# Batch 0's v as one contiguous load, loads in the order q, k, v, and 512-column gap filling

## The chip, the cores and the metric

The kernel runs on one core of one Trainium2 chip. Its time is the device time of one execution in microseconds (us). Three executions of the kernel before gave 324.27, 326.92 and 322.95 us, a median of 324.27.

Engines are TensorE (PE in the profile; its weight loads are PEld), VectorE (DVE), ScalarE (ACT), GpSimd (POOL) and SyncE (SP). Each takes its instructions in order. DMAs are issued here from two queues: GpSimd's, which can change a type on the way (float32 to bf16), and SyncE's.

## What is computed

An attention whose keys and values are first mixed block by block, and then a two-layer network on its result. Sizes: 4 batches, 8 heads, a sequence of 768 in 8 blocks of 96, head dimension 64; 3072 tokens of 512, a hidden layer of 2048.

```python
P = sort_net                                   # (4, 8, 8, 8)
for _ in range(5):                             # Sinkhorn
    P = exp(P - max(P, -1))
    P = P / (sum(P, -1) + 1e-9)
    P = P / (sum(P, -2) + 1e-9)
k_sorted = einsum('bhij,bhjcd->bhicd', P, k_blocks)
v_sorted = einsum('bhij,bhjcd->bhicd', P, v_blocks)
attn = softmax(q_block @ k_sorted_block.T / 8)   # within each block of 96
x = (attn @ v_sorted_block)                      # to (3072, 512)
h = x @ w_in
out = (max(h, 0) + alpha * min(h, 0)) @ w_out
```

## The kernel before

**Order of the work.** Every operation is added to a graph (`G.add`, with an engine, a cost in ns, what it reads and writes, and a priority, the smaller the sooner). `_Graph.schedule` (L88) is a planner: it puts the operations of each engine into a fixed order by its own costs and due times, of DMAs too. Operations marked EITHER go to ScalarE or VectorE as it decides. `emit` writes that order out, with semaphore waits. On the chip each engine then follows its order, whatever the real times are. `fill` (L153) puts extra matmuls, whose result nobody reads, into the gaps that the plan has on TensorE up to a given time (`warm`, L817).

**Loads.** GpSimd issues in this order: v, k, q of batch 0 (768 KB each as they land in bf16), the two weight matrices (`w_in` in four parts, `w_out` in two), zeroing of QN, then k, q (eight pieces, QN) and v of later batches. For batch 0, `load_v` (L362) reads v in halves: 128 partitions, each with 3072 numbers, from source rows taken in two interleaved sets of 64.

**Batch 0.** Sinkhorn (L421) runs on 32 rows, with the exp on ScalarE (L431) and the rest on VectorE. `spread_k` (L445) lays P out on 128 partitions and masks it to a block matrix BDK; `spread_v` (L461) does so for BDV, whose third part belongs to batch 0's v. `prep_k` and `prep_q` (`pairs`, L477) multiply KS by BDK, or QS by an identity, 16 matmuls a unit for six units, which sorts and transposes at once; the copies to KT and QTz follow (L318 is the copy on either engine). `conv_v` (L512) reorders v in SBUF from VST to VD in four pieces, and `prep_v` (L518) sorts it in eight units of 16 matmuls over 64 partitions each, with BDV; its copies go to VS.

**Later batches.** q comes by DMA into QN and is transposed by DMA on SyncE's queue (`turn_q`, L349, L351) into QTz, of which there are two; the next batch's QN loads wait for those transposes. v is sorted on TensorE by `sort_v` (L538, L545), written to DRAM and read back in another order (`turn_v`, L554; L556 and L563, SyncE's queue) into VS, in two halves. k goes the way of batch 0.

**Attention and FFN.** `attention` (L571) does one block g of 32: scores (L594, or L591 for later batches), their negated maximum (L598), scores again with the maximum subtracted (L622 or L612, and L604), exp to Esb (L632), the product with VS (L640), division (L647, L650), transposition into xT (L659). `ffn1` (L671, matmuls L679) and `ffn2` (L699, matmuls L711) work on finished tokens between the blocks, by priority.

Of the kernel before, what the change touches and what calls it, by code (L numbers as in the profile page):

```python
# [7 lines left out]
AP = bass.AP  # L8
# [48 lines left out]
class _Graph:  # L57
# [30 lines left out]
    def schedule(self):  # L88
# [22 lines left out]

        free = dict.fromkeys(ENGS, 0.0)
        dma_free = 0.0
        order = {e: [] for e in ENGS}
# [38 lines left out]
    def fill(self, make, unit, first, before):  # L153

        out, last = [], self.ops[first].end + 300
        for op in self.order["pe"]:
            n = int((op.start - last) * 0.9 / unit)
            if op.start < before and n > 2:
                x = _Op("pe", lambda e, n=n: make(e, n), n * unit, 0.0, None, len(self.ops))
                x.start, x.end = last, last + n * unit  # L160
                x.deps.add(first)
                self.ops.append(x)
                out.append(x)
            out.append(op)
            last = max(last, op.end)
        for pos, op in enumerate(out):
            op.pos = pos
        self.order["pe"] = out
# [69 lines left out]
def bass_sinkhorn_attn__then__act_prelu_kernel(  # L238
# [37 lines left out]
    selk = sb("selk", [32, 4, 128], F32)  # L276
    selv = sb("selv", [32, 3, 128], F32)
    dtmp = sb("dtmp", [128, 64], F32)
    dsel = sb("dsel", [128, 8], F32)
    BDK = sb("BDK", [128, 4, 128], BF16)  # L280
    BDV = sb("BDV", [128, 3, 128], BF16)
    epst = sb("epst", [32, 8], F32)
# [30 lines left out]
    BANK_H = [(psH, x * 512, 1024, [("psH", x, 0), ("psH", x, 1)]) for x in range(2)]  # L313
    BANK_O = [(psO, x * 512, 1024, ["psO%d" % x]) for x in range(2)]
    BANKS0 = [BANK_P] + BANK_H + BANK_O

# [45 lines left out]
    def load_v(b, prio):  # L362
        if b == 0:
            G.add(POOL, lambda e: e.dma_start(
                AP(VST, 0, [[6144, 128], [1, 3072]]),
                AP(v.tensor, 0, [[3072, 2], [6144, 64], [1, 3072]])),
                load_us, w=[("VST", 0), ("VST", 1)], prio=prio, dma=(d_v[0], 0))
            return
        G.add(POOL, lambda e: e.dma_start(
            AP(VST, (b % 2) * 64 * 6144, [[6144, 64], [1, 6144]]),  # L370
            AP(v.tensor, b * HB, [[6144, 64], [1, 6144]])),
            load_us, w=[("VST", b % 2)], prio=prio, dma=(d_v[b], 0))


    def consts():
# [29 lines left out]
        red(mvj[:, :], AP(identf, 0, [[128, 128], [1, 8], [8, 16]]), "mvj")  # L405
        for t, w, ld, name in ((selk, 16, 512, "selk"), (selv, 8, 384, "selv")):
            G.add(ACT, lambda e, t=t, w=w, ld=ld: copy(e, AP(t, 0, [[ld, 32], [w, 32], [1, w]]),
                                                       AP(identf, 0, [[128, 32], [1, 32], [0, w]])), 600,
                  r=["identf"], w=[name], prio=-66)
        G.add(ACT, lambda e: copy(e, AP(selv, 256, [[384, 32], [64, 2], [8, 8], [1, 8]]),  # L410
                                  AP(identf, 0, [[128, 32], [0, 2], [1, 8], [0, 8]])), 300,
              r=["identf"], w=["selv2"], prio=-66)
        return ib.idx
# [47 lines left out]
    def spread_v(x, prio):  # L461
        G.add(PE, lambda e: e.matmul(psYP[:, 1, 0:64], AP(selv, x * 128, [[384, 32], [1, 128]]), P32[:, :]),
              500, r=["P"] + (["selv2"] if x == 2 else ["selv", ("xT", 1)]), w=PSP, prio=prio)
        G.add(DVE, lambda e: e.tensor_tensor(
            out=AP(dtmp, 0, [[64, 128], [8, 8], [1, 8]]), in0=AP(psYP, 512, [[1024, 128], [8, 8], [1, 8]]),
            in1=AP(mvj, 0, [[8, 128], [0, 8], [1, 8]]), op=AluOpType.mult), 210,
            r=PSP + ["mvj"], w=["dtmp"], prio=prio)
        G.add(DVE, lambda e: e.reduce_sum(dsel[:, :], AP(dtmp, 0, [[64, 128], [8, 8], [1, 8]]),
                                          axis=AxisListType.X), 200, r=["dtmp"], w=["dsel"], prio=prio)
        G.add(DVE, lambda e: e.tensor_tensor(  # L470
            out=AP(BDV, x * 128, [[384, 128], [8, 16], [1, 8]]),
            in0=AP(mvh, 0, [[16, 128], [1, 16], [0, 8]]),
            in1=AP(dsel, 0, [[8, 128], [0, 16], [1, 8]]), op=AluOpType.mult), 290,
            r=["dsel", "mvh"], w=[("BDV", x)], prio=prio)

# [22 lines left out]
    def prep_k(b, u, prio, bank=BANK_P):  # L498
# [8 lines left out]
        if b == 0 and u == 1:  # L507
            G.add(DVE, lambda e: e.tensor_copy(AP(KT[0], 48, [[ld, 128], [bk, 32], [1, 16]]),
                                               AP(KT[0], 0, [[ld, 128], [bk, 32], [1, 16]])), 500,
                  r=[("KT", 0, 0), ("KT", 0, 1)], w=["KTpad"], prio=prio + 1)  # L510

    def conv_v(u, prio):  # L512
        o = AP(VD, 16 * u * 64, [[6144, 128], [64, 16], [1, 48]])
        i = AP(VST, 16 * u, [[6144, 128], [1, 16], [64, 48]])
        G.add(EITHER if u == 3 else ACT, lambda e: copy(e, o, i), {"act": 1520, "dve": 890},
              r=[("VST", 0), ("VST", 1)] + ["P"] * (u == 3), w=[("VD", u)], prio=prio)

    def prep_v(u, prio, bank):  # L518
        t, off, row, keys = bank

        def f(e):
            inst = None
            for dd in range(8):
                for th in range(2):
                    inst = e.matmul(AP(t, th * 64 * row + off + dd * 64, [[row, 64], [1, 64]]),
                                    AP(VD, th * 64 * 6144 + (8 * u + dd) * 64, [[6144, 64], [1, 64]]),
                                    AP(BDV, th * 64 * 384 + 256 + th * 64, [[384, 64], [1, 64]]))
            return inst
        G.add(PE, f, 8 * 33, r=[("VD", u // 2), "VD0", ("BDV", 2)], w=keys, prio=prio)
        o = AP(VS[0], 8 * u, [[64 * 65, 112], [65, 64], [1, 8]])  # L530
        i = AP(t, off, [[row, 112], [1, 64], [64, 8]])
        G.add(EITHER, lambda e: copy(e, o, i), {"act": 685, "dve": 690}, r=keys + [("VS1", 0)], w=[("VS", 0)] if u == 0 else
              [("VSu", u)], prio=prio)
# [4 lines left out]
    def sort_v(bs, c, prio):  # L538
        row, rows, keys = (bs[0] % 2) * 64, 64 * len(bs), [("VST", b % 2) for b in bs]

        def f(e):
            inst = None
            for b in bs:
                r0 = (b % 2) * 64
                inst = e.matmul(AP(psYP, r0 * 1024 + 512, [[1024, 64], [1, 512]]),  # L545
                                AP(BDV, r0 * 384 + (b // 2) * 128 + r0, [[384, 64], [1, 64]]),
                                AP(VST, r0 * 6144 + c * 512, [[6144, 64], [1, 512]]))
            return inst
# [19 lines left out]

    first_y = []

    def attention(g, prio):  # L571
        b, i = g // NB, g % NB
        n, m = b % 2, g % 2
        far = b > 0
# [9 lines left out]
        def s1(e):  # L584
# [11 lines left out]
            return inst  # L596
        G.add(PE, s1, t_pe(*[(96, 96)] * 8), r=kt_keys + qt_keys, w=banks_s, prio=prio)
        G.add(DVE, lambda e: e.tensor_reduce(  # L598
            AP(nm[m], 0, [[8, 96], [4, 2], [1, 4]]), AP(psX, 0, [[1024, 96], [512, 2], [96, 4], [1, 96]]),
            AxisListType.X, AluOpType.max, negate=True), t_dve(768), r=banks_s, w=[("nm", m)], prio=prio)  # L600

# [6 lines left out]
        def s2(e):  # L608
# [17 lines left out]
            for h4 in range(4):  # L626
# [3 lines left out]
        G.add(PE, s2, t_pe(*[(192, 96), (96, 96), (96, 96)] * 4), r=kt_keys + qt_keys + [("nm", m), "identb"],  # L630
              w=banks_s, prio=prio)
        G.add(ACT, lambda e: e.activation(  # L632
            AP(Esb[m], 0, [[768, nk], [384, 2], [1, 384]]), AP(psX, 0, [[1024, nk], [512, 2], [1, 384]]),
            ACTF.Exp, scale=0.125), t_act(768), r=banks_s, w=[("Esb", m)], prio=prio)

        def o(e):
# [6 lines left out]
            return inst  # L643
        op = G.add(PE, o, t_pe(*[(65, 96)] * 8), r=vs_keys + [("Esb", m)], w=banks_o, prio=prio)
        if g == 1:
            first_y.append(op)
        G.add(DVE, lambda e: e.reciprocal(AP(rec[m], 0, [[8, 96], [4, 2], [1, 4]]),  # L647
# [75 lines left out]


    load_v(0, -98)
    load_k(0, -97)
    load_q(0, -96)
    ident_op = consts()
    sinkhorn()
    for u in range(4):  # L730
        conv_v(u, -50)
    bank = 0
    spread_k(0, -48)
    spread_v(2, -47.5)
    for name, count, prio in (("k", 6, -47), ("v", 8, -45), ("q", 6, -46)):
        for u in range(count):
            x = BANKS0[bank % 5]
            bank += 1
            prep_k(0, u, prio, x) if name == "k" else prep_v(u, prio, x) if name == "v" else prep_q(u, prio, x)
    for p in range(4):  # L740
# [76 lines left out]
    def warm(e, n):  # L817
        inst = None
        for _ in range(n):
            inst = e.matmul(psYP[:, 0, 0:128], identb[:, :], identb[:, :])  # L820
        return inst
    G.fill(warm, 56, ident_op, first_y[0].start)
    if __import__("os").environ.get("SCHED"):
# [39 lines left out]
```

## Time and profile before

| | us |
|---|---|
| median of three executions | 324.27 |
| the profiled execution | 322.16 |
| its span, first to last instruction | 320.4 |
| TensorE busy (matmul) in it | 274.1 |
| VectorE, ScalarE, GpSimd busy | 170.9, 139.3, 34.6 |
| first sorting matmul of P (L447) starts | 38.84 |
| first product with VS (L640) starts | 64.13 |
| first FFN matmul (L679) starts | 68.69 |

Stages, from the busy time of each engine in windows of the span:

| window, us | TensorE busy | granted clock | GB/s moved |
|---|---|---|---|
| 0 to 10 | 6.36 | 1.00 | 114 |
| 10 to 20 | 5.23 | 0.90 | 206 |
| 20 to 30 | 0.00 | 0.50 | 195 |
| 30 to 40 | 1.16 | 0.50 | 196 |
| 40 to 50 | 6.72 | 0.67 | 167 |
| 60 to 65 | 4.95 | 0.77 | 31 |
| 70 to 75 | 5.00 | 0.50 | 22 |
| 90 to 120 | 28.79 | 1.00 | 145 |
| 120 to 160 | 34.13 | 0.91 | 134 |
| 160 to 200 | 39.69 | 1.00 | 89 |
| 250 to 300 | 49.64 | 1.00 | 33 |

In the profile an entry such as "VD<-VST" is what is written and what is read; "x6" counts instructions; a bracket gives the idle time before an instruction and what ended it. In the DMA views the last number is the time from issue to landing. The time slices give the busy share in tenths; PEclk is the granted TensorE clock in tenths of full speed, and GB/s counts the bytes as they are written. The chain of waits is followed back from the last instruction, at each step to what released it.

### The profile page before, as it was taken

What the parts mean: (1) busy time and instruction counts of PE and PEld (TensorE: products, weight loads), DVE (VectorE), ACT (ScalarE), POOL (GpSimd) and SP (SyncE); (2) the same over time, 40 slices, a digit from 0 to 9 for tenths busy, and PEclk for the clock granted to TensorE, in tenths of its full rate; (3) what the DMA queues carried; (4) which work ended last, traced back from release to release, by engine and by line L of the source; (5) the groups of instructions that cost most, each with busy time, mean ns of one, the idle gap of its engine ahead of it and who ended that gap; (6) DMA issues with size and microseconds to landing.
All of it is one profiled execution on the core that took longest, in us unless ns stands there. A gap on an engine that the chain in (4) does not pass through costs nothing.

```text
span 320.4 us, 6603 instructions
## 1 busy us (share of the span) xinstructions
PE 274.1 (86%) x2871; PEld 182.7 (57%) x2904; DVE 170.9 (53%) x349; ACT 139.3 (43%) x265; POOL 34.6 (11%) x53
## 2 busy tenths in 40 slices
PE   5900176989899893999999999999999999999996
PEld 5800165866666551766666666666666666655542
DVE  5100443375676523677675666677656666554420
ACT  4000542242577652576545445544444544444421
POOL 8920050000061006200000000000000000000000
PEclk9965565685999997899999999999999999999999
DMA  6999999226999999949937991000000000000012
GB/s 89 208 196 205 192 168 164 44 27 39 142 124 140 132 199 166 178 101 52 170 45 136 106 110 46 35 34 2 35 33 35 33 36 33 35 33 35 33 55 78
DMA packets 66589, 29.81 MB, mean 93 GB/s; under 512 B 58032, under 2 KB 62144, under 8 KB 66368
## 3 DMA queue, kind: packets, MB, share of 16 engines
q1 hardware_dynamic: 41552, 15.75, 35.1%
q0 software_dynamic: 25008, 13.64, 32.2%
q8 instruction: 23, 0.38, 0.6%
q14 instruction: 6, 0.05, 0.1%
HBM read 29.64 MB, written 8.65 MB: 119 GB/s over the span
## 4 chain that ended last, share of the span: by engine, by line
PE 77%; DMA 12%; SPq 3%; issue 3%; DVE 2%; ACT 1%; POOLq 0%
PE psH L679 26%; PE psYP L711 21%; DMA VST<-in_v_dram 10%; PE psS L604 4%; PE psO L640 4%; SPq L351 3%; PE psS L711 3%; PE psS L591 3%; PE psS L612 3%; PE psYP L485 2%; PE psYP L545 2%; DMA VS<-v_sorted_dram 2%; PE psYP L820 2%; PE psO L659 2%; PE psS L622 1%
## 5 line engine op out<-in xcount | busy, mean ns | idle before, releaser
L690 DVE SCALAR_TENSOR_TENSOR hT<-t,omaT,psH 128x384 bf16<-128x384 f32 (+1 forms) x144 | 80.5, 566 | 60.6 <-ACT t L687 59.3
L679 PE MATMUL psH<-xT,w_in_bf 128*128 128x384 bf16 (+1 forms) x576 | 103.1, 314 | 0.0
L687 ACT ACTIVATE t<-psH 128x384 f32<-128x384 f32 (+1 forms) x144 | 64.7, 453 | 68.2 <-PE psH L679 67.4
L711 PE MATMUL psYP<-w_out_bf,hT 128*128 128x512 bf16 x304 | 80.1, 382 | 2.4 <-issue 1.0
L679 PEld LDWEIGHTS psH<-xT,w_in_bf 128*128 128x128 bf16 x576 | 50.8, 100 | 26.5 <-issue 1.8
L711 PEld LDWEIGHTS psYP<-w_out_bf,hT 128*128 128x128 bf16 x336 | 30.9, 98 | 27.8 <-issue 1.2
L632 ACT ACTIVATE Esb<-psS 96x768 bf16<-96x768 f32 (+1 forms) x31 | 25.0, 807 | 33.8 <-PE psS L604 33.4
L598 DVE TENSOR_REDUCE nm<-psS 96x8 bf16<-96x768 f32 x31 | 29.5, 950 | 9.6 <-PE psS L591 6.3
L344 POOL DMA_DIRECT2D QN<-in_q_dram x24 | 19.8, 857 | 62.5 <-DMA QTz<-QN 62.5
L604 PE MATMUL psS<-identb,nm 96*96 96x96 bf16 (+1 forms) x248 | 23.7, 214 | 0.0
L604 PEld LDWEIGHTS psS<-identb,nm 96*96 96x96 bf16 (+1 forms) x248 | 21.7, 129 | 2.0
L447 PE MATMUL psYP<-P,selk 32*128 32x64 f32 x8 | 2.5, 406 | 23.6 <-DVE P L442 23.6
L820 PE MATMUL psYP<-identb 128*128 128x128 bf16 x229 | 19.1, 256 | 3.6 <-ACT identb L318 3.6
L640 PEld LDWEIGHTS psO<-VS,Esb 96*96 96x96 bf16 (+1 forms) x248 | 15.9, 129 | 11.0 <-DMA VS<-v_sorted_dram 5.7
L650 DVE TENSOR_TENSOR xq<-psO,rec 96x512 bf16<-96x512 f32 x31 | 21.3, 687 | 1.1
L640 PE MATMUL psO<-VS,Esb 96*96 96x65 bf16 (+1 forms) x248 | 16.7, 213 | 5.9 <-DMA VS<-v_sorted_dram 5.4
L820 PEld LDWEIGHTS psYP<-identb 128*128 128x128 bf16 x229 | 16.9, 116 | 4.1 <-ACT identb L318 3.6
L612 PE MATMUL psS<-QTz,KT 128*96 128x192 bf16 x96 | 19.1, 254 | 0.1
L318 ACT ACTIVATE outstg<-psYP 128x512 f32<-128x512 f32 x21 | 12.5, 597 | 8.8 <-PE psYP L711 8.8
L447 PEld LDWEIGHTS psYP<-P,selk 32*128 32x128 f32 x8 | 1.8, 275 | 24.4 <-DVE P L442 23.8
L318 ACT ACTIVATE VD<-VST 128x768 bf16<-128x768 bf16 x3 | 4.5, 1490 | 25.7 <-DMA VST<-in_v_dram 25.7
L433 DVE TENSOR_REDUCE rs<-P 32x8 f32<-32x64 f32 x5 | 1.0, 208 | 26.6 <-ACT P L431 26.6
(117 smaller groups left out, 234.4 us busy)
## 6 DMA issues: line engine op xcount, KB each, us to landing
out_dram<-outstg SPq DMA_DIRECT2D x24, 256.0 KB, 2.0
VST<-in_v_dram POOLq DMA_DIRECT2D x4, 768.0 KB, 33.1
KS<-in_k_dram POOLq DMA_DIRECT2D x4, 768.0 KB, 36.5
QN<-in_q_dram POOLq DMA_DIRECT2D x24, 96.0 KB, 6.2
v_sorted_dram<-VD SPq DMA_DIRECT2D x6, 384.0 KB, 4.4
VS<-v_sorted_dram SPq DMA_DIRECT2D x6, 384.0 KB, 10.1
w_in_bf<-in_moe_w_in_dram POOLq DMA_DIRECT2D x4, 512.0 KB, 42.1
w_out_bf<-in_moe_w_out_dram POOLq DMA_DIRECT2D x2, 1024.0 KB, 52.6
```

The lines of the kernel that those rows point to most:

```text
L344: G.add(POOL, lambda e, h=h: e.dma_start(AP(QN, h * 128 + (h // 4) * 64, [[6144, 128], [1024, 6], [1, 64]]), AP(q.tensor, b * HB + h * S * ...
L598: G.add(DVE, lambda e: e.tensor_reduce(AP(nm[m], 0, [[8, 96], [4, 2], [1, 4]]), AP(psX, 0, [[1024, 96], [512, 2], [96, 4], [1, 96]]), Axis ...
L604: return e.matmul(AP(psX, (p // 4) * 512 + (p % 4) * 96, [[1024, nk], [1, 96]]), AP(nm[m], p, [[8, 96], [0, nk]]), AP(identb, 0, [[128, 96 ...
L612: e.matmul(AP(psX, (h4 // 2) * 512 + (h4 % 2) * 192, [[1024, 96], [1, 192]]), AP(KT[n], (h4 * 8 + i) * 96, [[ld, 128], [1, 96]]), AP(QTz[n ...
L632: G.add(ACT, lambda e: e.activation(AP(Esb[m], 0, [[768, nk], [384, 2], [1, 384]]), AP(psX, 0, [[1024, nk], [512, 2], [1, 384]]), ACTF.Exp ...
L640: inst = e.matmul(AP(psZ, hp * 512 + h4 * 68, [[1024, 96], [1, 65]]), AP(Esb[m], pos(h4, hp) * 96, [[768, nk], [1, 96]]), AP(VS[n], ((hp * ...
L650: G.add(DVE, lambda e: e.tensor_tensor(out=AP(xq[m], 0, [[512, 96], [256, 2], [64, 4], [1, 64]]), in0=AP(psZ, 0, [[1024, 96], [512, 2], [6 ...
L679: inst = e.matmul(AP(psH, hb * 512, [[1024, 128], [1, n]]), AP(w_in_bf, kt * DFF + ft * 128, [[KT_TILES * DFF, 128], [1, 128]]), AP(xT, kt ...
L687: G.add(ACT, lambda e: e.activation(AP(t1[tb], 0, [[384, 128], [1, n]]), AP(psH, hb * 512, [[1024, 128], [1, n]]), ACTF.Relu, scale=-1.0), ...
L690: G.add(DVE, lambda e: e.scalar_tensor_tensor(out=AP(hT, ft * RING + tok % RING, [[FT_TILES * RING, 128], [1, n]]), in0=AP(t1[tb], 0, [[38 ...
L711: inst = e.matmul(AP(bank[0], bank[1], [[row, 128], [1, 512]]), AP(hT, ft * RING + tok % RING, [[FT_TILES * RING, 128], [1, 128]]), AP(w_o ...
L820: inst = e.matmul(psYP[:, 0, 0:128], identb[:, :], identb[:, :])
```

## The change

- `load_v` reads batch 0's v with the source as 128 rows of 3072 in their order. v is then laid out as k is, so that `prep_v` sorts it with BDK, over all 128 partitions in one matmul, each second column of BDK being taken; BDV's third part, its selector and its `spread_v` go.
- The loads of batch 0 are issued in the order q, k, v; q's preparation comes first in priority, then k's, the scores of the first two blocks, v's conversion (all four pieces now on either engine), and v's sorting, which uses four PSUM banks.
- In the planner GpSimd starts at 400 ns, so that its order changes a little. `fill` begins at 5000 ns, fills any gap in which a matmul has room, with 512-column matmuls costed at 215 ns (128 columns and 56 ns before), and ends before the first `prep_v` that writes the bank the filler writes, where it ended before the second block's product with VS.

```diff
@@ schedule
         free = dict.fromkeys(ENGS, 0.0)
+        free["pool"] = 400.0
@@ fill
-            n = int((op.start - last) * 0.9 / unit)
-            if op.start < before and n > 2:
+            n = int((op.start - max(last, 5000)) * 0.9 / unit)
+            if op.start < before and n > 0:
@@ load_v
-                AP(v.tensor, 0, [[3072, 2], [6144, 64], [1, 3072]])),
+                AP(v.tensor, 0, [[3072, 128], [1, 3072]])),
@@ conv_v
-        G.add(EITHER if u == 3 else ACT, lambda e: copy(e, o, i), {"act": 1520, "dve": 890},
-              r=[("VST", 0), ("VST", 1)] + ["P"] * (u == 3), w=[("VD", u)], prio=prio)
+        G.add(EITHER, lambda e: copy(e, o, i), {"act": 1520, "dve": 890},
+              r=[("VST", 0), ("VST", 1)], w=[("VD", u)], prio=prio)
@@ prep_v
                 for th in range(2):
                     inst = e.matmul(AP(t, th * 64 * row + off + dd * 64, [[row, 64], [1, 64]]),
-                                    AP(VD, th * 64 * 6144 + (8 * u + dd) * 64, [[6144, 64], [1, 64]]),
-                                    AP(BDV, th * 64 * 384 + 256 + th * 64, [[384, 64], [1, 64]]))
+                                    AP(VD, (8 * u + dd) * 64, [[6144, 128], [1, 64]]),
+                                    AP(BDK, th, [[512, 128], [2, 64]]))
-        G.add(PE, f, 8 * 33, r=[("VD", u // 2), "VD0", ("BDV", 2)], w=keys, prio=prio)
+        op = G.add(PE, f, 8 * 33, r=[("VD", u // 2), "VD0", ("BDK", 0)], w=keys, prio=prio)
+        if keys == ["psY"]:
+            first_y.append(op)
@@ attention: scores, maximum and exp of the first two blocks get the priority ps_
+        ps_ = g / 8 - 46.5 if g < 2 else prio
@@ the main part
-    load_v(0, -98)
+    load_q(0, -98)
     load_k(0, -97)
-    load_q(0, -96)
+    load_v(0, -96)
     ident_op = consts()
     sinkhorn()
+    spread_k(0, -48)
+    for u in range(6):
+        prep_q(u, -50, BANKS0[u % 5])
+    for u in range(6):
+        prep_k(0, u, -47, BANKS0[(u + 1) % 5])
     for u in range(4):
-        conv_v(u, -50)
-    bank = 0
-    spread_k(0, -48)
-    spread_v(2, -47.5)
-    for name, count, prio in (("k", 6, -47), ("v", 8, -45), ("q", 6, -46)):
-        for u in range(count):
...
+        conv_v(u, -45.5)
+    for u in range(8):
+        prep_v(u, -45, (BANK_O + [BANK_P, BANK_Y])[u % 4])
@@ warm
-            inst = e.matmul(psYP[:, 0, 0:128], identb[:, :], identb[:, :])
+            inst = e.matmul(psYP[:, 0, :], identb[:, :], AP(identb, 0, [[128, 128], [0, 4], [1, 128]]))
-    G.fill(warm, 56, ident_op, first_y[0].start)
+    G.fill(warm, 215, ident_op, first_y[0].start)
```

## The prediction, made before the change was run

> **What bounds the kernel now.** I read the page first: the time slices and the chain of work that ended last.
>
> ```profile
> PE   5900176989899893999999999999999999999996
> ...
> PEclk9965565685999997899999999999999999999999
> DMA  6999999226999999949937991000000000000012
> GB/s 89 208 196 205 192 168 164 44 27 39 142 124 140 132 199 166 178 101 52 170 45 136 106 110 46 35 34 2 35 33 35 33 36 33 35 33 35 33 55 78
> ```
>
> A slice is 8.0 us. From the eleventh on, the sixteenth apart, TensorE is full at a full clock, so a microsecond saved before that is a microsecond at the end unless a later wait takes it back. Slices 3 to 5 are nearly empty: they are the place to look. The chain in order of time:
>
> ```profile
> 1.32 32.47 DMA VST<-in_v_dram
> 33.80 1.50 ACT VD L318
> 38.84 0.68 PE psYP L447 x2
> ...
> 45.98 3.28 issue
> ...
> 54.61 1.92 issue
> ...
> 120.26 6.95 DMA VS<-v_sorted_dram
> 127.25 0.85 PE psO L640 x8
> ```
>
> It starts with batch 0's v, 32.5 us for 768 KB. The timeline shows what else that held up:
>
> ```profile
> 33.80 1.50 ACT L318 ACTIVATE VD<-VST 128x768 bf16<-128x768 bf16 x1 [25.74 <-DMA VST<-in_v_dram]
> 35.21 0.24 ACT L431 ACTIVATE P<-P 32x64 f32<-32x64 f32 x1
> 35.35 1.49 ACT L318 ACTIVATE VD<-VST 128x768 bf16<-128x768 bf16 x1
> ```
>
> ScalarE's fixed order has v's conversion ahead of Sinkhorn's fourth exp, so P, whose first three rounds end at 9.6 us at 1.81 us a round, is ready only at 38.8. Why the load is slow shows in the DMA issues, window by window:
>
> ```profile
> VST<-in_v_dram POOLq DMA_DIRECT2D x1, 768.0 KB, 32.5
> KS<-in_k_dram POOLq DMA_DIRECT2D x1, 768.0 KB, 35.2
> QS<-in_q_dram POOLq DMA_DIRECT2D x1, 768.0 KB, 37.9
> KS<-in_k_dram POOLq DMA_DIRECT2D x1, 768.0 KB, 53.7
> ```
>
> Issued at 1.32, 2.25, 3.16 and 13.10, they land at 33.8, 37.4, 41.1 and 66.8. k and q come 3.65 us behind their forerunner; v took nine times that. With all 16 DMA engines at work the slices show about 200 GB/s, 12.5 each; at 60 to 66 us the windows show 26 to 33, two engines' worth, while late loads are still landing. So v (source [[3072,2],[6144,64],[1,3072]]) runs on two engines, 393 KB on each, and every later load has a share that queues behind them.
> The Trainium skill, DMA: Bandwidth & Descriptors, "Why a DMA increments its semaphore by 16 and not by 1", says that the number of engines is the largest up to 16 that divides both slowest dimensions: 2 here. It also knows an exception in which GpSimd's copies use 16 anyway; by that v would land like k, and the change would gain nothing from its load. The 32.5 us speak against the exception.
>
> **The load.** As [[3072,128],[1,3072]] it has the form of k's and q's, 3.65 us. Two engines lose 393 − 49 = 344 KB each, at 49/3.65 = 13.5 KB per us 25.5 us. The fixed part is 32.5 − 393/13.5 = 3.3 us. So q lands at 1.32 + 3.3 + 3.65 = 8.3, k at 11.9, v at 15.6. What follows comes 25.5 us earlier: the last w_in at 28.1 (53.6), w_out at 37.6 (63.1), batch 1's k at 41.3.
>
> **Start to first FFN matmul** (L679 at 68.69 now). P no longer stands behind v: two more rounds of 1.81 from 9.6 give 13.2, up to 15 with q's copies (0.60 to 0.69 each) between; I take 14.3. spread_k to BDK took 38.84 to 40.36: 15.9. q's six units are then done. Six k units, copies 0.65 on two engines, with latency: KT at 18.5. First scores, reduction 0.95, second scores 0.9, exp 0.81: about 23. Conversions of v (1.5 on ScalarE, 0.8 on VectorE) fill in from 15.6 on. prep_v changes form: 128 matmuls contract over 128 rows, where now pairs of 64-row ones ran beside each other at 27 ns each (32 in 0.87 us). Nearest rows: L591, 128-row with 96 columns, 8 in 0.36 us, 45 ns; L604, 8 in 0.45. At 45 ns this is 5.8 us, at 27 it is 3.5; I take 45, since they can't pair. Its copies, 8 x 0.69 on two engines, 2.8 us, lie beside it. The first L640 comes at about 26. Add one stall like the "issue" ones, 3.28 and 1.92 us, which lie 128 matmuls apart while DMA is full: 0 to 5, I take 2. So 28; L679 followed L640 by 4.6: 32.6. Gain 36 us, between 32 and 40.
>
> **Small parts.** spread_v(2) goes: 0.69 us of TensorE, 0.74 of VectorE, 0.3 of ScalarE; all counted above as absent. The order q, k, v puts v last, 7.3 us behind q, where P and k's copies cover it; without them 7 us are at stake. The start of 400 in the planner and BDV's narrower rows move nothing by themselves. **Filler:** 170 matmuls of 128 columns ran at 12 per us first, 22 from 8 us on; four times as long that is 0.33, then 0.18 us each, planned at 0.215 for 90% of each gap. A planned gap of 3 us before q can overrun to about 4.2, ending near 9.2 and not 8: covered by Sinkhorn (14.3). If P were earlier, at most some 3 us. Warm against cold clock in this stretch: 0 to 3 us gain, taken as nil since copies set most of it.
>
> **Where a stall goes.** At 121.8 TensorE waits 5.4 us for batch 1's second half of VS, whose load stands behind batch 2's transposes on SP:
>
> ```profile
> 75.57 13.12 SPq L351 DMA_TRANSPOSE QTz<-QN  x6
> ...
> 107.60 12.61 SPq L351 DMA_TRANSPOSE QTz<-QN  x6
> 120.26 0.58 SPq L563 DMA_DIRECT2D VS<-v_sorted_dram  x1
> ```
>
> That chain is paced by queues: batch 1's q landed, transposes, GpSimd's next q loads from 90.81 to 97.39, their landing 5.2, transposes 12.7, VS 7.0. From the first transpose: 15.2 + 6.6 + 5.2 + 12.7 + 7.0 = 46.7 us; now it takes 51.7, because it also waits some 5 us for batch 0's last scores. Its start moves with the loads, not with the first matmul: 75.6 − 25.5 = 50.1, or 47 if all eight QN loads go ahead of batch 1's v, which waits on GpSimd for the conversions (till about 21; they now end at 39.6). VS then lands at 94 to 97. TensorE arrives at 121.8 − 36 = 85.8. The stall becomes 8 to 11 where it was 5.4: +2.8 to +5.6. I take 2.8, as TensorE's order can put more FFN work ahead of it. Batch 1's v lands near 51, where its first sort (86.4 − 36 = 50.4) wants it: 0 to 3, inside that stall. Sum: −36 + 2.8 = −33.2.
>
> **The numbers.** Against the profiled execution (320.4 span, 1.8 around it, 322.16) this gives 289.0. The median shown is 2.1 higher; I predict **290**.
>
> **Rivals.**
> 1. *The queue chain does not bind.* If the planner puts VS ahead of batch 2's transposes, the stall disappears: −36 − 5.4 = −41.4, 281 to 283. For: those two stand only 10 us apart in SP's order. Against: the orders of SP are made by the same costs. 0.2.
> 2. *It binds harder.* v_sorted's second write also falls behind the transposes, as its sort waits for v while scores come sooner: another 4.4 us of landing and 0.5 to 1 of issue, or a start 4 us slower: −26, about 298. 0.22.
> 3. *The load isn't what is slow*, 33 us being the bandwidth for all 6.5 MB queued. Then q's transposes still start at 75.6, the stall hands all back: 318 to 324. Against: 26 GB/s at the end. 0.04.
> 4. *Slower: the clock.* At 70 to 78 us TensorE was busy 2.00 of every 2.00 us and had a clock of 0.50. Fill now ends before v's preparation, in front of the FFN. Half clock costs half of the work done under it; to be slower than before it has to last over 2 x 33 = 66 us, 80 for 2%; the longest busy stretch seen is about 9. Worth 330. 0.03.
>
> The skill's TensorE: Matmul & The Clock Gate, Part 1, has the full clock back after about 3.4 us of sustained work; the eight busy microseconds at 0.50 differ from that. By it, rival 4 couldn't be.
>
> My case holds 0.51. 80% lie in **279 to 301**, which reaches from rival 1 with a 2 us better start to rival 2 with a 3 us worse one. What can be told from no change is about 2%, 6.5 us. Faster 0.93 (my case, rivals 1 and 2), within 2% 0.04, slower 0.03.
>
> **What would show it.** Right: landings near 8, 12 and 16 us; P by 15; L447 before 17; first L679 at 30 to 35; no stretch at 26 to 33 GB/s before 60 us; transposes from 47 to 51; one wait for VS of 8 to 11 us before 100. Wrong: v landing after 30 (the engines' reading falls); first L679 after 40 (filler, the 128-row matmuls or code loading were underpriced); a wait for VS above 15 or none; half clock for tens of microseconds in the FFN.

## The result, and the profile after

The changed kernel takes 302.88 us (median of four, 301.19 to 303.34) against 324.42 of the kernel before: 0.9326 of it, 95% interval 0.9265 to 0.9386, so 21.5 us less. 290 was predicted, with 279 to 301 as the range: the gain is there, but more than a third of what was forecast is missing. The profiled execution has a span of 299.5 us, 20.9 less than before.

First the landings of the first three loads (DMA issues of the changed kernel in the window 1 to 4 us; the last number is from issue to landing):

```profile
QS<-in_q_dram POOLq DMA_DIRECT2D x1, 768.0 KB, 6.6
KS<-in_k_dram POOLq DMA_DIRECT2D x1, 768.0 KB, 9.7
VST<-in_v_dram POOLq DMA_DIRECT2D x1, 768.0 KB, 13.0
```

Issued at 1.30, 1.96 and 2.81, they land at 7.9, 11.7 and 15.8; 8.3, 11.9 and 15.6 were predicted. Batch 1's k lands at 41.2 (41.3). The page's time slices, 7.5 us each:

```profile
PE   5996999999960049999999999999999999999995
...
PEclk9997559999995559999999999999999999999999
...
GB/s 121 207 206 189 215 169 214 177 166 105 129 189 88 188 191 27 125 73 155 40 131 149 64 84 35 38 2 35 37 35 37 11 27 35 37 35 35 37 70 70
```

The hole at the beginning is gone. There is a new one in slices 12 to 15, which the kernel before does not have in that size. TensorE's timeline shows its edges, with the idle time and its cause in the bracket:

```profile
87.28 0.52 PE L593 MATMUL psS<-KT,QTz 128*96 128x96 bf16 x8
108.65 0.63 PE L548 MATMUL psYP<-VST,BDV 64*64 64x512 bf16 x2 [20.84 <-DMA VST<-in_v_dram]
```

L548 is the sort of later batches' v (L545 before); this is the first one for batches 2 and 3. It does not wait for VS, as the prediction had it, but for batch 3's v in VST. GpSimd's timeline says why that v is late:

```profile
20.50 0.68 POOL L361 DMA_DIRECT2D KS<-in_k_dram  x1
21.35 1.06 POOL L371 DMA_DIRECT2D VST<-in_v_dram  x2 [0.17 <-issue]
66.15 6.62 POOL L346 DMA_DIRECT2D QN<-in_q_dram  x8 [43.73 <-DMA QTz<-QN]
86.66 6.56 POOL L346 DMA_DIRECT2D QN<-in_q_dram  x8 [13.89 <-DMA QTz<-QN]
93.14 0.62 POOL L371 DMA_DIRECT2D VST<-in_v_dram  x1
```

Before, GpSimd issued batch 3's v at 104.72 and batch 3's QN pieces at 122.88:

```profile
39.91 0.55 POOL L369 DMA_DIRECT2D VST<-in_v_dram  x1 [22.15 <-DVE dtmp L449]
...
45.33 0.57 POOL L359 DMA_DIRECT2D KS<-in_k_dram  x1 [1.83 <-PE psYP L485]
...
104.72 0.55 POOL L369 DMA_DIRECT2D VST<-in_v_dram  x1 [7.33 <-PE psYP L545]
122.88 4.13 POOL L344 DMA_DIRECT2D QN<-in_q_dram  x5 [17.61 <-DMA QTz<-QN]
```

Now the pieces come first, at 86.66, and they wait for batch 2's transposes to have read QN. The v load behind them goes out at 93.14, and lands 15.5 us later. At the top of the queue two others have changed places too: batch 2's k (20.50, before 45.33) now goes before batch 1's v (21.35, before 39.91). SyncE's timeline, for the other half of that chain:

```profile
46.60 17.41 SPq L353 DMA_TRANSPOSE QTz<-QN  x6
...
75.47 8.86 SPq L353 DMA_TRANSPOSE QTz<-QN  x6
84.37 0.62 SPq L559 DMA_DIRECT2D v_sorted_dram<-VD  x1
...
94.26 0.45 SPq L559 DMA_DIRECT2D v_sorted_dram<-VD  x1
107.56 0.34 SPq L566 DMA_DIRECT2D VS<-v_sorted_dram  x1
```

Before, the first v_sorted write stood ahead of batch 2's transposes (107.60):

```profile
95.41 0.53 SPq L556 DMA_DIRECT2D v_sorted_dram<-VD  x1
```

Now it stands behind them, and so does everything that follows from it.

### The profile page after: what moved, and what is told of

Same layout as the page of the kernel before. It is cut to its first block, busy times and chain, and to the rows that moved or that the text cites. A ratio compares the mean times of both kernels' runs of the same rounds, so it can differ in the third digit from the quotient of the medians.

```text
span 299.5 us, 6232 instructions
## 1 busy us (share of the span) xinstructions
PE 267.3 (89%) x2705; PEld 167.4 (56%) x2705; DVE 173.2 (58%) x351; ACT 134.8 (45%) x259; POOL 35.0 (12%) x53
## 3 DMA queue, kind: packets, MB, share of 16 engines
q0 software_dynamic: 24112, 13.63, 37.3%
## 4 chain that ended last, share of the span: by engine, by line
PE 79%; DMA 7%; DVE 5%; SPq 2%; POOL 2%; ACT 2%; issue 1%; POOLq 0%
PE psH L679 27%; PE psYP L711 24%; DMA VST<-in_v_dram 5%; PE psS L606 4%; PE psO L642 4%; PE psS L711 3%; PE psS L593 3%; PE psS L614 3%; PE psYP L548 2%; SPq L353 2%; POOL QN L346 2%; PE psO L659 2%; PE psYP L484 2%; DMA QTz<-QN 1%; PE psS L624 1%
## 5 line engine op out<-in xcount | busy, mean ns | idle before, releaser
L711 PE MATMUL psYP<-w_out_bf,hT 128*128 128x512 bf16 x336 | 87.0, 383 | 0.4 <-DVE hT L690 0.4
L548 PE MATMUL psYP<-VST,BDV 64*64 64x512 bf16 x36 | 9.9, 413 | 21.1 <-DMA VST<-in_v_dram 20.8
L346 POOL DMA_DIRECT2D QN<-in_q_dram x24 | 20.4, 887 | 57.6 <-DMA QTz<-QN 57.6
L320 ACT ACTIVATE VD<-psYP 64x512 bf16<-64x512 f32 (+1 forms) x14 | 8.3, 594 | 30.3 <-PE psYP L548 30.1
L614 PE MATMUL psS<-QTz,KT 128*96 128x192 bf16 x96 | 18.5, 248 | 0.1
L642 PE MATMUL psO<-VS,Esb 96*96 96x65 bf16 (+1 forms) x248 | 16.7, 213 | 0.4 <-ACT Esb L634 0.2
L548 PEld LDWEIGHTS psYP<-VST,BDV 64*64 64x64 bf16 x36 | 2.5, 104 | 25.7 <-DMA VST<-in_v_dram 21.0
L819 PE MATMUL psYP<-identb 128*128 128x512 bf16 x32 | 10.5, 476 | 3.3 <-ACT identb L320 3.3
L614 PEld LDWEIGHTS psS<-QTz,KT 128*96 128x96 bf16 x96 | 11.9, 124 | 2.7 <-DVE nm L600 0.2
L593 PEld LDWEIGHTS psS<-KT,QTz 128*96 128x96 bf16 x192 | 11.5, 125 | 2.8
## 6 DMA issues: line engine op xcount, KB each, us to landing
QN<-in_q_dram POOLq DMA_DIRECT2D x24, 96.0 KB, 11.7
```

The costliest lines, as they stand in the source:

```text
L320: return e.activation(o, i, ACTF.Copy) if e is nc.scalar else e.tensor_copy(o, i)
L346: G.add(POOL, lambda e, h=h: e.dma_start(AP(QN, h * 128 + (h // 4) * 64, [[6144, 128], [1024, 6], [1, 64]]), AP(q.tensor, b * HB + h * S * ...
L614: e.matmul(AP(psX, (h4 // 2) * 512 + (h4 % 2) * 192, [[1024, 96], [1, 192]]), AP(KT[n], (h4 * 8 + i) * 96, [[ld, 128], [1, 96]]), AP(QTz[n ...
L642: inst = e.matmul(AP(psZ, hp * 512 + h4 * 68, [[1024, 96], [1, 65]]), AP(Esb[m], pos(h4, hp) * 96, [[768, nk], [1, 96]]), AP(VS[n], ((hp * ...
L711: inst = e.matmul(AP(bank[0], bank[1], [[row, 128], [1, 512]]), AP(hT, ft * RING + tok % RING, [[FT_TILES * RING, 128], [1, 128]]), AP(w_o ...
```

## The experiments

Two theories were set against each other. Theory 1: the missing part is the order of two queues, GpSimd's and SyncE's, which the planner has turned round. Theory 2: the DMA engines are full there, and whoever is first will be late. Beside that, the reading that an outermost dimension of 2 puts a load on two DMA engines was to be tried by itself, and the filler.

### Batch 3's v ahead of its QN pieces

After planning, the start of the eight QN pieces is set behind that of v, so that GpSimd's order alone changes:

```diff
     total = G.schedule()
+    pool = G.order["pool"]
+    v3 = [o for o in pool if o.prio == -9][0]
+    for j, o in enumerate([o for o in pool if o.prio == -2]):
+        o.start = v3.start + 1 + j
+    pool.sort(key=lambda o: (o.start, o.idx))
...
```

> The changed kernel, with one thing moved: on GpSimd's queue batch 3's v (L371) goes ahead of batch 3's eight QN pieces instead of behind them. Theory 1 (queue order): the 20.8 us wait of TensorE at 88 us is there because that v load stands behind QN pieces that wait for transposes; now it is issued near 77 and lands by 87, the wait falls under 3 us. The transposes still stand ahead of batch 1's v_sorted writes on SP (84.4 and 94.3 us), so the product with VS then waits 9 to 13 us and the time is 291 to 295; if nothing is behind it, 281 to 284. Theory 2 (the DMA engines are full there, 15.5 us to landing whoever is first): the load lands past 95 all the same, and the time stays at 298 or above.

Measured: 305.53 us (305.12 to 307.41), 2.7 longer than the change, against 291 to 295 expected. The load itself did as expected: out at 76.28, landed 8.3 us later. But TensorE then stood still in another place:

```profile
94.61 0.63 PE L548 MATMUL psYP<-VST,BDV 64*64 64x512 bf16 x2 [5.12 <-ACT VD L320]
118.20 0.85 PE L642 MATMUL psO<-VS,Esb 96*96 96x65 bf16 x8 [16.71 <-DMA VS<-v_sorted_dram]
```

The first wait is a new one: the copy of the new sort writes VD, which batch 1's v_sorted write, late on SP, has not yet read. The second is the product with VS: 16.7 us where 9 to 13 were expected, and batch 2's transposes, which hold up the v_sorted writes, took 13.63 us in this run where the change has 8.86. The 20.8 us are found again as 5.1 + 16.7. The time lies in theory 2's range, but its reason is not what this shows: the load was in time. It is the second half of the queue chain that decides.

### Batch 2's transposes behind batch 1's VS loads, alone

```diff
...
+    last = [o for o in sp if o.prio == 5.25][-1]
+    for j, o in enumerate([o for o in sp if 10 <= o.prio <= 12.5 and o.dur == 2500]):
+        o.start = last.start + 1 + j
+    for j, o in enumerate([o for o in pool if o.prio in (-2, -9)]):
+        o.start = last.start + 10 + j
...
```

> The changed kernel with batch 2's transposes behind batch 1's VS loads on SP's queue, and batch 3's v left behind batch 3's QN pieces on GpSimd's. Theory 1 (one chain through both queues, each move alone only shifts the wait): the transposes end near 102, QN pieces go out to 111, v lands at 118 to 126 and TensorE waits 30 us or more for it: 308 to 320, slower than the change. Rival (the two moves act by themselves, each with its own gain): 283 to 296.

Measured: 310.81 us (309.57 to 310.87), in the range of theory 1 and outside the rival's. TensorE's wait is again for batch 3's v:

```profile
116.59 0.63 PE L548 MATMUL psYP<-VST,BDV 64*64 64x512 bf16 x2 [27.70 <-DMA VST<-in_v_dram]
```

It was 27.7 us, and not 30: the transposes ended at 98.9 instead of 102.

### Both together

```diff
...
+    last = [o for o in sp if o.prio == 5.25][-1]
+    for j, o in enumerate([o for o in sp if 10 <= o.prio <= 12.5 and o.dur == 2500]):
+        o.start = last.start + 1 + j
+    for j, o in enumerate([o for o in pool if o.prio == -2]):
+        o.start = last.start + 10 + j
...
```

> The changed kernel with two things moved: batch 3's v ahead of batch 3's QN pieces on GpSimd's queue, and batch 2's six transposes (L353) behind both of batch 1's VS loads (L566) on SP's queue. Theory 1 (queue order, both queues): no wait over 4 us is left between 60 and 120 us, and the time is 279 to 285. Theory 2 (full DMA engines): waits for VST or VS of 10 us and more remain, 295 or above.

Measured: **282.80 us** (281.32 to 283.54), 0.8707 of the kernel before (0.8653 to 0.8761). TensorE's two waits for DMA are nearly gone:

```profile
89.63 0.40 PE L548 MATMUL psYP<-VST,BDV 64*64 64x512 bf16 x2 [1.25 <-DMA VST<-in_v_dram]
97.73 0.55 PE L642 MATMUL psO<-VS,Esb 96*96 96x65 bf16 x8 [1.55 <-DMA VS<-v_sorted_dram]
```

The four runs side by side, in us:

| | transposes ahead of VS (as planned) | transposes behind VS |
|---|---|---|
| QN pieces ahead of v (as planned) | 302.88 | 310.81 |
| QN pieces behind v | 305.53 | 282.80 |

Neither move gains anything alone, both together gain 20.1 us. That is the sign of one chain through two queues: each link that is taken out hands the wait to the next. Theory 2 falls, with 282.8 against its 295 or more. Full DMA engines do play a part in the size of the waits, though: the same load of batch 3's v took 8.3 us to land in the first of these runs, 12.0 in this one and 15.5 in the changed kernel. This version beats both kernels; below it is the one "with both queues mended".

### The load order turned back

```diff
-    load_q(0, -98)
+    load_v(0, -98)
     load_k(0, -97)
-    load_v(0, -96)
+    load_q(0, -96)
```

> The changed kernel with batch 0's loads in the order v, k, q as before the change; all else stays, the planner works out the rest of the order. Theory 1 (the load order is what turned the later queues round): batch 1's v goes out before batch 2's k, batch 3's v before batch 3's QN pieces, and VS before batch 2's transposes; the 20.8 us wait goes, q lands near 15 and not 8 and costs 0 to 4 us at the start: 279 to 288. Rival (the order of the first three loads matters for the start alone): no gain, q last costs 0 to 4: 302 to 307.

Measured: 298.17 us (296.80 to 299.50); 279 to 288 was expected, so the size is missed. The orders did go back as theory 1 said: batch 3's v out at 74.88 and its QN pieces at 107.06, batch 2's transposes at 87.70, behind VS's second load at 87.08. But more is paid at the start than 0 to 4 us, and some of the waits stay:

```profile
22.19 0.37 PE L484 MATMUL psO<-BDK,KS 64*64 64x64 bf16 x6 [3.37 <-issue]
28.11 0.28 PE L526 MATMUL psO<-BDK,VD 128*64 128x64 bf16 x6 [1.99 <-issue]
...
91.48 0.64 PE L548 MATMUL psYP<-VST,BDV 64*64 64x512 bf16 x2 [4.63 <-DMA VST<-in_v_dram]
98.80 0.82 PE L642 MATMUL psO<-VS,Esb 96*96 96x65 bf16 x8 [5.29 <-issue]
```

The first FFN matmul comes at 37.82, 6.2 us later than with both queues mended (31.65): q's and k's preparation crowd together after P, and TensorE twice stands without anything that the profile shows. The two later waits are 9.9 against 2.8, 7.1 more (the last one ends when VS's second half lands, 87.08 + 11.6, whatever its label). 281.8 + 6.2 + 7.1 = 295.1, which is this run's span. So the order q, k, v is a gain at the start, and in the planner it is what turns the later queues round.

### The planner told what a transpose costs

```diff
-                free[e] = at + (600 if e == "pool" else 100)
+                free[e] = at + (600 if e == "pool" else 2000 if op.dur == 2500 else 100)
```

> The changed kernel; the planner alone is told that a transpose on SP's queue holds that queue for 2000 ns and not for 100 (the changed kernel's take 17.41 and 8.86 us for six). Theory 1 (the planner's wrong cost of the transposes is what spoils its order): it now puts batch 3's v ahead of its QN pieces and four of batch 2's six transposes still ahead of VS's second half; the wait at 88 goes, one of 3 to 10 us for VS stays: 283 to 293. Rival (the cost is not the cause): 300 or above.

Measured: 294.14 us (293.66 to 294.56), just above the range. GpSimd's order is mended (v at 77.94, QN pieces at 108.52), and the wait for VST is 1.55 us. SP's order is half mended:

```profile
88.30 4.35 SPq L353 DMA_TRANSPOSE QTz<-QN  x1
92.70 1.34 SPq L559 DMA_DIRECT2D v_sorted_dram<-VD  x1
94.08 6.10 SPq L353 DMA_TRANSPOSE QTz<-QN  x3
100.22 0.59 SPq L566 DMA_DIRECT2D VS<-v_sorted_dram  x1
```

Five of the six transposes still stand ahead of VS's second load, and TensorE waits 8.6 us for it (the fifth transpose is at 85.07, ahead of these lines). The cost of 100 ns is one cause of the bad order; a planner that takes whatever can start first still lets batch 2's transposes go ahead of a load that batch 1 waits for.

### The load alone

The kernel before, with v in two DMAs of 64 partitions each, the same layout:

```diff
-                AP(VST, 0, [[6144, 128], [1, 3072]]),
-                AP(v.tensor, 0, [[3072, 2], [6144, 64], [1, 3072]])),
+            for th in range(2):
...
+                    AP(VST, th * 64 * 6144, [[6144, 64], [1, 3072]]),
+                    AP(v.tensor, th * 3072, [[6144, 64], [1, 3072]])),
...
```

> The kernel before with one thing changed: batch 0's v is loaded by two DMAs of 64 partitions each, in the same layout, so that each has 64 as its slowest dimension. Theory 1 (two engines held everything up): v lands by 9 us, k and q by 12 and 16, everything later 25 us sooner; the first FFN matmul comes at 30 to 38 instead of 68.7, the wait for VS grows from 5.4 to 8 to 12, and the time is 284 to 294. Rival (the gain of the change comes from its order, priorities and filling): within 5 us of before, 319 or above.

Measured: 294.37 us (293.44 to 295.64), just above the range, and 8.5 us faster than the whole change. v has landed by 8.5 us, k and q near 12 and 16. The first FFN matmul comes at 40.13, later than 30 to 38. P is complete at 13.5, but TensorE is at its filler matmuls until about 15.6 and takes P up only at 15.56; q's preparation comes last, and there are two "issue" stalls of 2.72 and 1.24 us. How much each of them costs was not tried. The wait for VS did not grow: it is 1.79 us. The run differs from the kernel before in more than the load, since the planner, given two loads, made another order, with batch 2's transposes behind VS's second load, where they stood ahead of it (107.60 and 120.26 before):

```profile
89.30 0.32 SPq L564 DMA_DIRECT2D VS<-v_sorted_dram  x1
...
95.26 9.13 SPq L351 DMA_TRANSPOSE QTz<-QN  x6
```

What the load gains in the old order of the queues was not measured.

### The old load in the changed kernel

A first run split source and copy into two halves that follow each other.

```diff
-                AP(v.tensor, 0, [[3072, 128], [1, 3072]])),
+                AP(v.tensor, 0, [[196608, 2], [3072, 64], [1, 3072]])),
```

> The changed kernel with batch 0's v read by the same rows into the same places, but with the source and so the copy in two halves outermost ([[196608, 2], [3072, 64], [1, 3072]]). Theory 1 (an outermost 2 puts a load on two DMA engines): q lands at 8, k at 12 as in the changed kernel, v only at 38 to 43; the first FFN matmul comes at 52 to 58 and not at 31.6, and as the later loads are some 25 us later too, the time is 322 to 334. Rival (what the load's form does is small, the order of the loads matters): v lands by 25, 300 to 308.

Measured: 303.08 us (302.56 to 305.68), with v 12.8 us from issue to landing: in the rival's range, not in theory 1's. Every engine has the same order as in the change. An outermost 2 as such is thus not slow. Here the two halves join on (196608 is 64 x 3072), so that they describe the same run of rows as the changed kernel's source; that they are put together again on the way to the DMA engines fits the landing, but was not seen. The second run took the old source as it was, whose two halves interleave:

```diff
-                AP(v.tensor, 0, [[3072, 128], [1, 3072]])),
+                AP(v.tensor, 0, [[3072, 2], [6144, 64], [1, 3072]])),
```

> The changed kernel with the source of batch 0's v as it was before the change ([[3072, 2], [6144, 64], [1, 3072]]), all else and every engine's order as in the changed kernel; v's rows stand in another order in SBUF, so batch 0 mixes other rows of v. (a_two joined its two halves into one run of rows again and so measured the changed kernel a second time.) Theory 1 (an outermost 2 puts a load on two DMA engines): q lands at 8, k at 12, v only at 38 to 43; the first FFN matmul comes at 52 to 60 and not at 31.6, the later loads are some 25 us later too: 322 to 336. Rival (the form of the load matters little): v lands by 25, 300 to 308.

Measured: 327.64 us (326.79 to 331.59), in theory 1's range, and 1.0072 of the kernel before (1.0041 to 1.0103). The landing, and what waits for it:

```profile
VST<-in_v_dram POOLq DMA_DIRECT2D x1, 768.0 KB, 38.5
```

```profile
42.18 1.07 PE L526 MATMUL psO<-BDK,VD 128*64 128x64 bf16 x32 [24.08 <-DVE VD L320]
```

q and k, which are ahead of it, land within 0.5 us of the change; v itself takes 38.5 us where the same bytes took 13.0, and the first FFN matmul comes at 56.2. At 60 to 66 us the DMA engines move 26 GB/s, as they did before the change, with a busy share of 0.13 to 0.16, which is 2.1 to 2.6 of 16 engines. With nothing but the load undone, the whole gain of the change is gone. That the rows are interleaved is not the reason: the two DMAs of "The load alone" read the same rows in the same steps of 6144, and theirs have landed by 8.5 us.

### The filler

The kernel with both queues mended, without `G.fill`:

> The kernel with both queues mended (282.8 us), without the filler matmuls. Theory 1 (the filler does little, since copies, P and landings set the start): the first FFN matmul at 31 to 34, the time 0 to 3 us longer, 282 to 286. Rival a (a warm clock at the start is worth its price): 4 us or more longer, 287 or above. Rival b (the filler stands in the way): shorter, below 281.

Measured: 282.57 us (280.92 to 283.52), against 282.80 with the filler: no difference in the time. TensorE's busy time in the first 20 us falls from 15.23 to 7.09 us. The start does become slower: the first product with VS comes at 28.39 where the filler has 25.94, the first FFN matmul at 34.10 where it has 31.65.

```profile
34.10 1.46 PE L679 MATMUL psH<-xT,w_in_bf 128*128 128x192 bf16 x8
```

Part of this shows already in q's preparation, where 32 matmuls take 1.06 us at 8.56 and 0.69 with the filler. The 2.45 us are gone again later: TensorE then has no wait for batch 3's v (1.25 with the filler) and one of 1.13 us for VS (1.55), and both profiled executions have a span of 281.8 us. So theory 1 holds for the time: the filler is worth some 2.5 us at the start, and the shorter waits give back 1.7 of them; where the rest is made up is not shown.

### Batch 1's v ahead of batch 2's k

```diff
+    v1 = [o for o in pool if o.prio == -19][0]
+    k2 = [o for o in pool if o.prio == -12][0]
+    k2.start = v1.start + 1
...
```

> The kernel with both queues mended (282.8 us), and on GpSimd's queue batch 1's v ahead of batch 2's k as it was before the change. Theory 1: v lands 3.6 us sooner (52.5 and not 56.4), its sort and the two v_sorted writes behind it come sooner; the waits of 1.25 and 1.55 us at 88 and 97 shrink, 279 to 282. Rival (TensorE is the limit there already, its order is fixed): 282 to 284.

Measured: 286.85 us (286.22 to 288.62), 4 us longer than without it; both theories missed. The first sort of batch 1 starts at 57.99 as before (58.02): v was not what it waited for. In this run, though, the transposes start at 50.01 and not at 46.82, batch 2's QN pieces go out at 69.48 and not at 66.35, and batch 3's v, issued at the same time (77.57), takes 14.9 us to land where it took 12.0; TensorE waits 4.1 us for it. The transposes start 3.2 us later because the last of batch 1's QN pieces lands 30.3 us after its issue where it took 27.1; why it does, although it stands ahead of the two loads that changed places, was not tried.

## Why the prediction was off

**What held.** The reading of the load: two engines and 25.5 us of backlog. The landings of q, k, v, w_out and batch 1's k are within 0.5 us of what was worked out (the last w_in came at 26.4, 1.7 us early), and the undone load gives the time of before. P was ready at 12.9 (14.3), the first product with VS came at 25.89 (28), the first FFN matmul at 31.59 (32.6): the gain up to there was 37.1 us where 36 were taken. The stall like the "issue" ones came, 1.49 us of the 2. That the filler was worth nothing held for the end; at the start it was worth 2.5 us in the mended version, which was taken as nil.

**Sizes that were wrong without deciding it.** The 128-row matmuls of prep_v, taken at 45 ns, ran at 22 (32 in 0.69 us): a price too high by 3 us. Its reason, that they can't pair, did not show: at a granted clock of 0.50, 32 of them took 1.07 us without the filler, and 32 of the paired ones 1.06 us before the change (at 50.48; a row of 32 in 0.87 us is not in that trace). So the first product came 2.1 us early, of which 1.1 were lost again before the first FFN matmul: that the start fits to 1 us is in part luck. And 289.0 with 2.1 for the median is 291, not 290. In rival 4, TensorE was busy 1.78 of the last two microseconds before 78, and not 2.00.

**What failed** is the step "Where a stall goes", and in it the sentence that the stall becomes 8 to 11 us. The gain was carried through the queues as they stood in the trace of before: the chain ended at VS on SP's queue, and batch 3's v, on GpSimd's, was not in it, since before it was issued 18 us ahead of batch 3's QN pieces. But the change goes through a planner. With v last of the first three loads it put batch 1's v behind batch 2's k, batch 2's transposes ahead of the v_sorted writes, and batch 3's QN pieces ahead of its v; with v first again, and nothing else undone, it puts them back. So the wait was for another tile, on another queue, and 20.8 us long; of a wait for VS there was none, which the prediction had named as a sign of being wrong. The sum with the measured terms: −37.1 at the start, +20.8 for the new wait, −5.4 for the old one, which is no longer waited for, −21.7; the span fell by 20.9.

**The rivals.** Rival 2 had the one half of this, the v_sorted write behind the transposes, and came nearest in time (298). Its mechanism is there, though hidden in the changed kernel: its price shows only once batch 3's v is moved, as 16.7 us; that its 298 lies nearest to the time is luck. The sentence that the order of the loads costs nothing as long as P covers v was right for the start and wrong for the queues. Rival 1's queue order is that of the mended version: 281 to 283 was its price, 282.8 the time. Rivals 3 and 4 did not happen.

**Part by part,** in us: the load alone, with the order that the planner made for it, −30.0 (324.4 to 294.4); the rest of the change with its queues mended a further −11.6 (to 282.8), with the first FFN matmul 8.5 earlier (from 40.13 to 31.65); the turned queues +20.1 (to 302.9); the filler 0 in the mended version. As the order of the queues differs between these kernels, the first two figures are not those of the load and of the start alone.

## What to carry to other kernels

Where an order is planned, an edit at one end can turn queues round far away: before the gain of the first part is written down, go through every in-order queue for pairs that may change places, loads of later stages above all. When a wait that was removed comes back elsewhere, look for the chain and take out both links: here each alone gave nothing, and both gave 20 us. And look at a load's outermost dimension: 2, with halves that interleave, where 64 or 128 was to be had cost 25 us, for that load and for all behind it.

## What was not expected of the hardware

**Half clock under a full load.** Busy time of each engine in windows of the changed kernel (PE first, then PEld, DVE, ACT and POOL; the granted clock stands third from the end):

```profile
22.00:24.00 2.00, 0.51 (x20) 0.35 (x18) 0.86 (x2) 1.31 (x2) 0.42 (x1) 1.00 1.24 203
...
28.00:30.00 2.00, 1.82 (x25) 1.49 (x25) 1.05 (x3) 1.30 (x2) 0.00 (x0) 0.50 1.24 207
30.00:32.00 2.00, 2.00 (x17) 1.76 (x17) 1.63 (x4) 0.49 (x1) 0.00 (x0) 0.50 1.25 207
...
40.00:42.00 2.00, 2.00 (x16) 1.31 (x16) 1.80 (x6) 0.33 (x1) 0.00 (x0) 0.50 2.28 151
42.00:44.00 2.00, 2.00 (x15) 1.34 (x13) 1.04 (x2) 0.60 (x2) 0.00 (x0) 0.63 2.42 158
```

Two microseconds with TensorE busy for only 0.51 come shortly before the clock falls, and it stays down from about 26 to 43 us, with TensorE busy all the time from 30 on. The matmuls agree: eight of the first FFN layer take 1.46 us at 31.59 and 0.83 at 44.85. The Trainium skill, TensorE: Matmul & The Clock Gate, Part 1, has about 3.4 us of sustained work for that; here it took at least 12. By our estimate some 16 us at half clock cost at most 8 us. How much of that the end would see is not shown: in the mended version the 2.45 us that the start lost without the filler were not seen at the end. Two of the four executions without the filler have a mean granted clock of 1.00 and took 282.95 and 282.19 us, between the other two (283.52 and 280.92). This is no proof either, since a record of 1.00 can stand where matmuls are slow: it does at 8 to 10 us in that version's profile, where 32 matmuls took 1.06 us.

**Transposes.** Six of them held SP's queue for 17.41, 8.86 and 8.70 us in one run, and for 13.63 us in the second place of another. Most take little: of the 18 in the changed kernel the median is 1.34 us and the longest 8.23. What sets their time was not tried.
